# Inverse product over the 32 places on 64-row halves, with the correction added in the third stage

## The chip, the cores and the metric

One core of one Trainium2 chip runs the kernel. The metric is the device time of one execution in microseconds (us), as the median of several runs. The profile comes from one execution taken by the hardware profiler; its span (first to last instruction) is a little shorter than the time of that execution.

## The reference

The input x has 2048 rows of 576 numbers. After a layer norm the kernel adds three things: x itself, a spectral filter, and a gated linear unit.

```python
def _A_ref(x, w_r, w_i):
    X = rfft2(x, axes=(-2, -1))
    X = X * (w_r + 1j * w_i)
    return irfft2(X, s=(S, D), axes=(-2, -1))

def _B_ref(x, w_gate, w_up, w_down):
    g = einsum("bsd,df->bsf", x, w_gate)
    u = einsum("bsd,df->bsf", x, w_up)
    return einsum("bsf,fd->bsd", sigmoid(g) * u, w_down)

xn = _layernorm(x, axis=-1)
return x + _A_ref(xn, A_w_r, A_w_i) + _B_ref(xn, B_w_gate, B_w_up, B_w_down)
```

S is 2048, D is 576 and F is 4608. The setup scales w_r and w_i by 64.

## The kernel before

All matmuls run on numbers that are split in two: a high part with 12 bits and the rest, the low part. A product of two numbers is then three matmuls: high by high, high by low, low by high. Where the text speaks of a main sum and a correction, the correction is the part that comes from a matrix's low part.

The gated unit makes nearly all the work. It is cut into 36 blocks of 128 columns of F ("units"), and the 2048 rows into two halves of 1024, which run one after the other. A unit in `unit` has seven products of seven matmuls of 128x512 (`prod`, L710). Beside them run the down products `ps` (L1060) and `po` (L849) with 12 matmuls of 128x288 to a group.

The spectral filter is spread over the second half of the kernel. One step of it is done after each of the seven products of a unit; a step lasts some 2.7 us. The two-dimensional transform is done in three stages, and each task of a stage is a generator whose `yield`s are the ends of its steps:

- Stage one, `phase1b`, 16 tiles: the transform over the columns and then over the 64 slow places of the 2048 rows. It writes the result, high and low part apart, to `sc1` in the chip's main memory.
- Stage two, `phase2`, 16 tasks of 4.1 steps' distance: each takes four spectral rows (two pairs), transforms over the 32 fast places (`pb`, L566), multiplies by the filter `w` (the tile `ri`) and transforms back over the 32 places (`pc`, L591). The filtered numbers are split in `zh` and `zl` (128 partitions x 2 x 290). The result is evicted to `u` by ScalarE (L593) and written to `sc2` by a DMA on SyncE's queue (L594).
- Stage three, `phase3`, 16 tiles of 4.5 steps' distance: it loads a tile of `sc2` (L599), splits it into `uh` and `ul` (L612, L613), transforms back over the 64 places (`py`, L619), then over the columns (`pz`, `pe`), and adds the result to the output rows.

The constant `bm` holds four 128x128 matrices of stage two, two for the forward direction and the high and low part of the inverse one. In the inverse product the matmuls are full: for each of the two halves of `zh` and `zl`, three matmuls of 128 rows and 290 columns, so six in one task:

```python
pc = pair(f"pc{i}")
for j in range(2):
    for n, (k, m) in enumerate(((2, zh), (2, zl), (3, zh))):
        nc.tensor.matmul(pc[:, j, :NQ], bm[:, k, :], m[:, j, :], start=n == 0, stop=n == 2)
```

What sets the order: `pair` gives out two double PSUM banks in turn, to `pb`, `pc`, the sums `ps` and `po` and the products of stage three alike. A product can take its bank only when the one before it in that bank was evicted. TensorE takes its matmuls in the order in which they were laid out. All DMAs of the filter, as well as the weight pieces `w` (L323) and the down factors `wf` (L957), are issued on SyncE's queue, which works in order: a trigger that waits holds those behind it. In the second half the weights have one buffer, in which a piece is replaced as soon as its product is done and is read again one unit later. Instructions that are marked `keep_in_program_order` keep their place; others can be laid out earlier or later by the framework as their operands and buffers come free.

Of the kernel before, what the change touches and what calls it, by code (L numbers as in the profile page):

```python
# [9 lines left out]
F32 = mybir.dt.float32  # L10
F32R = mybir.dt.float32r
I32 = mybir.dt.int32
AF = mybir.ActivationFunctionType
# [3 lines left out]
P = 128  # L17
S, D, F = 2048, 576, 4608
KD = D // 2 + 1
NQ = KD + 1  # L20
# [36 lines left out]
def _split(m):  # L57

    def r12(v):
        b = np.ascontiguousarray(v, np.float32).view(np.uint32).astype(np.uint64)  # L60
        b = ((b + 0x7FF + ((b >> 12) & 1)) & 0xFFFFF000).astype(np.uint32)
        return b.view(np.float32)

    hi = r12(m.astype(np.float32))
    lo = r12((m - hi.astype(np.float64)).astype(np.float32))
    return hi, lo


def _cplx(m):

    return np.block([[m.real, m.imag], [-m.imag, m.real]])


def _constants():
    out = {}

    mid = np.arange(HD) - (D - 1) / 2
    ang = 2 * np.pi * mid[:, None] * KOF[None, :] / D
    t = np.zeros((P, 2, 5, NQ), np.float32)
    for e, v in ((0, np.cos(ang)), (1, -np.sin(ang))):  # L80
        m = np.where(FREQ, v - (v.mean(0) if e == 0 else 0), 0.0)
        hi, lo = _split(m)
        for part, w in ((0, hi), (1, lo)):
            t[:, e, 2 * part] = w[:P]
            t[:, e, 2 * part + 1] = w[P:2 * P]
        t[:KR, e, 4] = np.concatenate([hi[2 * P:], hi[2 * P:], lo[2 * P:]])
    out["cf"] = t.reshape(P, 10 * NQ)


    s1 = np.arange(N1)  # L90
    k1 = np.arange(N1)
    am = np.zeros((P, N2, 2, P), np.float32)
    ai = np.zeros((P, N2, 2, P), np.float32)
    for s2 in range(N2):
        ph = 2 * np.pi * (((N2 * s1[:, None] + s2) * k1[None, :]) % S) / S
        m = _cplx(np.exp(-1j * ph))
        am[:, s2, 0], am[:, s2, 1] = _split(m)
        m = _cplx(np.exp(1j * ph).T)
        ai[:, s2, 0], ai[:, s2, 1] = _split(m)
    out["am"] = am.reshape(P, N2 * 2 * P)  # L100
    out["ai"] = ai.reshape(P, N2 * 2 * P)


    s2 = np.arange(N2)
    ph = 2 * np.pi * ((s2[:, None] * s2[None, :]) % N2) / N2
    bh, bl = (v.reshape(2, N2, N1).transpose(1, 0, 2).reshape(N1, N1) for v in _split(_cplx(np.exp(-1j * ph))))
    none = np.zeros_like(bl)
    bi = _cplx(np.kron(np.exp(1j * ph), np.eye(2)))
    at = np.arange(P).reshape(2, N2, 2)
    bi = bi[at.transpose(2, 0, 1).ravel()][:, at.transpose(1, 0, 2).ravel()]  # L110
    b = np.stack([np.block([[bh, bl], [bh, none]]), np.block([[bl, bh], [none, bh]]), *_split(bi)], 1)
    out["bm"] = b.reshape(P, 4 * P)


    a = np.where((KOF == 0) | (KOF == HD), 1.0, 2.0)[:, None] / (D * S) * FREQ[:, None]
    ang = 2 * np.pi * KOF[:, None] * (QTR[None, :] + 0.5) / D
    t = np.zeros((P, 2, 2, 2, HQ), np.float32)
    r = np.zeros((P, 2, HD), np.float32)
    for e, m in ((0, a * np.cos(ang)), (1, a * np.sin(ang))):
        m[KOF == (HD, 0)[e]] = 0.0  # L120
        hi, lo = _split(m)
        for k, rows in enumerate((slice(0, P), slice(NQ - P, NQ))):
            t[:, e, k, 0], t[:, e, k, 1] = hi[rows], lo[rows]
        h, l = np.zeros((2, FR, HD), np.float32)
        for s, v in ((h, hi), (l, lo)):
            v = v[P:NQ - P]
            o = ODD[P:NQ - P]
            s[o, (1 - e) * HQ:(2 - e) * HQ] = v[o]
            s[~o, e * HQ:(e + 1) * HQ] = v[~o]
        r[:3 * FR, e] = np.concatenate([h, h, l])  # L130
    out["di"] = np.concatenate([t.reshape(P, 8 * HQ), r.reshape(P, 2 * HD)], 1)
    out["id"] = np.eye(P, dtype=np.float32)
    return out
# [6 lines left out]
def _layout(x, w_r, w_i, w_gate, w_up, w_down):  # L140

    ks = np.concatenate([np.arange(KT * P), np.tile(np.arange(KT * P, HD), 4)])
    w = np.stack([w_gate[COLS], w_up[COLS]]).reshape(2, 2, HD, NF, P)[:, :, ks]
    w = w[[1, 1, 0, 0], [0, 1, 1, 0]].reshape(4, KT + 1, P, NF, P).transpose(3, 2, 0, 1, 4)
    v = np.stack([w_r, w_i])[:, :, KOF].reshape(2, N2, 2, N2 // 2, 2, NQ).transpose(3, 2, 1, 0, 4, 5)
    v = np.broadcast_to(v[:, :, None], (N2 // 2, 2, 2, N2, 2, 2, NQ))
    x = x.reshape(S, D)[ROWS][:, COLS]
    xt = x[:, np.argsort(COLS)].reshape(NT, P, 2, HD)
    xt = np.stack([xt[:, :, 0], xt[:, :, 1, ::-1]], 2)
    xt = xt[..., ks].reshape(NT, P, 2, KT + 1, P).transpose(0, 4, 2, 3, 1)  # L150
    xg = x.reshape(NT, P, 2, HD)[TPP:, ..., ks].reshape(2, TPC, P, 2, KT + 1, P).transpose(0, 3, 5, 4, 1, 2).reshape(2, 2, P, (KT + 1) * CW)
    lay = {"x": x.reshape(NT, P, D), "xt": xt.reshape(NT, P, 2 * (KT + 1) * P), "xg": xg, "ri": v.reshape(N2 // 2, P, 4 * NQ),
           "w": w.reshape(NF, P, 4 * (KT + 1) * P), "wd": w_down[:, COLS].reshape(NF, P, D)}
    return {k: np.ascontiguousarray(a) for k, a in lay.items()}
# [9 lines left out]
def spectral_glu_kernel(ctx: ExitStack, tc: tile.TileContext, x, xt, xg, ri, w_in, w_down, out):  # L164
# [3 lines left out]
    def f32(ap):  # L168
        return ap.bitcast(F32)
# [6 lines left out]
    def pair(name):  # L176
        return ps.tile([P, 2, 512], F32, tag="pp", name=name, bufs=2)
# [21 lines left out]

    rowd = tc.dram_tile([2, NT, P], F32, name="rowd")  # L200
    sc1 = tc.dram_tile([2, N2 * P, NQ], F32, name="sc1")
    sc2 = tc.dram_tile([N2 * P, NQ], F32, name="sc2")
    spill = tc.dram_tile([TPP * P, D], F32, name="spill")
    wsp = [tc.dram_tile([P, NX * 5 * P], F32, name=f"wsp{f}") for f in range(NF)]
    wdsp = [tc.dram_tile([P, 2 * D], F32, name=f"wdsp{f}") for f in range(NF)]
# [342 lines left out]

    def phase2(i):
        pool, bm, zz = R["pool"], R["bm"], R["zz"]  # L550
        kl = 2 * i
        x2 = pool.tile([P, 2, 2, NQ], F32R, tag="x2", name=f"x2{i}", bufs=2)
        nc.sync.dma_start(f32(x2), sc1.rearrange("a (q h kl) n -> (a q) h kl n", h=2, kl=N2)[:, :, kl:kl + 2])
        w = pool.tile([P, 2, 2, NQ], F32, tag="ri", name=f"ri{i}", bufs=2)
        nc.sync.dma_start(w.rearrange("p a j n -> p (a j n)"), ri[i])
        wr, wi = w[:, 0], w[:, 1]
        yield
        yield
        yield
        half = slice(0, N1), slice(N1, P)  # L560
        s, c = (pool.tile([P, 2, NQ], F32, tag=f"s{h}", name=f"s{h}{i}") for h in range(2))
        for h, o in enumerate((s, c)):
            yield
            pb = pair(f"pb{i}_{h}")
            for j in range(2):
                nc.tensor.matmul(pb[:, j, :NQ], bm[:, h, :], x2[:, h, j, :], start=True, stop=True)  # L566
            nc.scalar.activation(o, pb[:, :, :NQ], AF.Copy)
        yield
        for h, o in enumerate((s, c)):
            nc.vector.tensor_tensor(s[half[h]], o[half[h]], o[half[1 - h]], op=OP.add)  # L570
        yield
        sw = pool.tile([P, 2, NQ], F32, tag="sw", name=f"sw{i}")
        for k in range(4):
            o, v = (slice(N2 * m, N2 * (m + 1)) for m in (k, k ^ 1))
            nc.scalar.activation(sw[o], s[v], AF.Copy, scale=-1.0 if k % 2 == 0 else 1.0)
        z = pool.tile([P, 2, NQ], F32, tag="z", name=f"z{i}")
        nc.vector.tensor_tensor(z, wr, s, op=OP.mult)
        yield
        nc.vector.tensor_tensor(sw, wi, sw, op=OP.mult)
        nc.vector.tensor_tensor(z, z, sw, op=OP.add)  # L580
        yield
        zh, zl = zz[i % len(zz)]
        nc.scalar.activation(zh, z, AF.Copy)
        yield
        nc.vector.tensor_tensor(zl, z, f32(zh), op=OP.subtract)
        yield
        yield
        pc = pair(f"pc{i}")
        for j in range(2):
            for n, (k, m) in enumerate(((2, zh), (2, zl), (3, zh))):  # L590
                nc.tensor.matmul(pc[:, j, :NQ], bm[:, k, :], m[:, j, :], start=n == 0, stop=n == 2)  # L591
        u = pool.tile([P, 2, NQ], F32, tag="u", name=f"u{i}", bufs=2)
        nc.scalar.activation(u, pc[:, :, :NQ], AF.Copy)  # L593
        nc.sync.dma_start(sc2.rearrange("(p kl) n -> p kl n", kl=N2)[:, kl:kl + 2], u)  # L594

    def phase3(t):
        pool, di, dr = R["pool"], R["di"], R["dr"]
        u = pool.tile([P, 2, NQ], F32, tag="u3", name=f"u3{t}", bufs=2)
        nc.sync.dma_start(u, sc2[2 * t * P:(2 * t + 2) * P].rearrange("(j p) n -> p j n", j=2))  # L599
        ai = pool.tile([P, 2, 2, P], F32R, tag="ai", name=f"ai{t}", bufs=2)  # L600
        load_r(ai, con["ai"][:, t * 4 * P:(t + 1) * 4 * P].rearrange("p (a h m) -> p a h m", a=2, h=2))
        if t < TPP:
# [3 lines left out]
            a = acc[t]  # L606
        yield
        yield
        yield
        uh = pool.tile([P, 2, NQ], F32R, tag="uh", name=f"uh{t}")  # L610
        ul = pool.tile([P, 2, NQ], F32R, tag="ul", name=f"ul{t}")
# [960 lines left out]
```

## Time and profile before

| what | value |
|---|---|
| median of 3 runs | 1375.23 us (1375.2 to 1375.95) |
| profiled execution, its own time | 1374.97 us |
| its span | 1373.2 us |
| stage two's `pc` matmuls, first to last start | 931.4 to 1101.9 us |
| stage three's `py` matmuls, first to last start | 1117.9 to 1340.1 us |
| evictions `u<-pc`, number and median | 16, 657 ns |

How to read the profile: a row of a group has the line of the kernel, the engine, the operation, the tile written and the tiles read, the shape (partitions x elements), the number of instructions, then the busy time in us and the mean time of one in ns, then the idle time of the engine ahead of them with what ended it. PE is TensorE's matmul, PEld its weight load, DVE VectorE, ACT ScalarE, SPq the DMA queue of SyncE. Rows of the timeline begin with the start and the length in us and end with the number of instructions merged. Rows of the waits end with us in total, times and the longest. The printed length of a matmul is modelled and overlaps the next one's; the time from start to start is what TensorE spends on it.

### The profile page before, as it was taken

Reading aid. Unit: us, or ns where it says so; the run is one execution under the profiler, and the core shown is the slowest. Engines: PE = TensorE matmul, PEld = TensorE weight load, DVE = VectorE, ACT = ScalarE, POOL = GpSimd, SP = SyncE. Lnnn points to the kernel's source line nnn. Section 1 sums busy time; section 2 is a strip of 40 time slices with the busy share of each in tenths; the row PEclk is TensorE's granted clock in tenths of the full one; section 3 lists DMA queues with packets and bytes.
Section 4 is the critical chain, followed back from the end, with each engine's and each line's share of the span. In section 5 each row is a group of like instructions: output and inputs, shape, how many; then the busy total and the mean of one; then the engine's idle time right before and its main releaser. Section 6 shows DMA issues by size and latency. Waiting matters only on the chain.

```text
span 1373.2 us, 20459 instructions
## 1 busy us (share of the span) xinstructions
PE 1360.3 (99%) x7656; PEld 1201.3 (87%) x7656; DVE 1069.9 (78%) x1555; ACT 776.1 (57%) x1228; POOL 3.3 (0%) x5
## 2 busy tenths in 40 slices
PE   8999999999999999999999999999999999999998
PEld 6888888888888888998888898988888888899887
DVE  7988888787878787999458668667878847777885
ACT  6644767677777767744245545447767634443432
POOL 0000000000000000000000000000000000000000
PEclk9999999999999999999999999999999999999999
DMA  7567786767676766595888878788989787775643
GB/s 258 200 250 284 267 317 251 287 261 267 266 268 260 274 262 256 212 316 179 286 261 269 264 242 251 217 310 304 307 303 314 231 280 254 225 236 174 197 147 87
DMA packets 127058, 346.56 MB, mean 252 GB/s; under 512 B 12816, under 2 KB 34096, under 8 KB 122224
## 3 DMA queue, kind: packets, MB, share of 16 engines
q1 hardware_dynamic: 125968, 343.94, 72.1%
q8 instruction: 61, 1.00, 0.3%
q10 hardware_dynamic: 992, 1.31, 0.3%
q14 instruction: 37, 0.30, 0.1%
HBM read 208.74 MB, written 136.46 MB: 251 GB/s over the span
## 4 chain that ended last, share of the span: by engine, by line
PE 88%; DVE 9%; ACT 2%; issue 1%; DMA 1%; DVEq 0%; ACTq 0%
PE pB L710 23%; PE ps L1060 22%; PE pE L710 15%; PE pA L710 14%; PE po L849 5%; PE pd L527 2%; PE pe L650 1%; PE pc L591 1%; PE py L619 1%; PE pa L543 1%; DVE acc L858 1%; PE pb L566 1%; DVE ys L825 1%; DVE w L284 1%; DVE hs L981 0%
## 5 line engine op out<-in xcount | busy, mean ns | idle before, releaser
L710 PE MATMUL pB<-X,w 128*128 128x512 f32 x1484 | 376.8, 392 | 1.0 <-ACT v L801 0.7
L1060 PE MATMUL ps<-wf,hs 128*128 128x288 f32 x2436 | 360.8, 295 | 1.2 <-DVE ev L655 1.2
L1060 PEld LDWEIGHTS ps<-wf,hs 128*128 128x128 f32 x2436 | 343.4, 188 | 16.4 <-ACT u L593 1.3
L710 PEld LDWEIGHTS pB<-X,w 128*128 128x128 f32 x1484 | 269.5, 188 | 52.5 <-ACT v L801 4.1
L710 PE MATMUL pE<-X,w 128*128 128x512 f32 x1064 | 269.3, 391 | 0.0
L710 PE MATMUL pA<-X,w 128*128 128x512 f32 (+1 forms) x1006 | 253.9, 389 | 0.7 <-ACT X L476 0.2
L710 PEld LDWEIGHTS pE<-X,w 128*128 128x128 f32 x1064 | 194.2, 188 | 35.7 <-DVE ys L803 0.4
L710 PEld LDWEIGHTS pA<-X,w 128*128 128x128 f32 x1006 | 182.3, 188 | 34.6 <-ACT g L798 0.9
L981 DVE TENSOR_TENSOR hs<-ys,hs 128x1024 fp32r<-128x1024 f32 (+1 forms) x105 | 124.7, 1187 | 39.6 <-ACT hs L978 38.5
L282 ACT ACTIVATE w<-raw 128x768 fp32r<-128x768 f32 (+1 forms) x106 | 100.3, 948 | 54.0 <-DVE raw L306 28.7
L978 ACT ACTIVATE hs<-ys 128x1024 fp32r<-128x1024 f32 (+1 forms) x105 | 108.0, 1028 | 24.7 <-PE ps L1060 19.1
L825 DVE TENSOR_TENSOR ys<-ys,g 128x1024 f32<-128x1024 f32 x67 | 81.9, 1223 | 3.7 <-DVE ys L823 0.5
L284 DVE TENSOR_TENSOR w<-raw,w 128x512 fp32r<-128x512 f32 (+1 forms) x106 | 81.7, 771 | 2.5 <-ACT w L282 2.3
L788 ACT ACTIVATE pB<-pA 128x512 f32<-128x512 f32 x68 | 39.6, 582 | 73.9 <-PE pA L710 71.6
L806 ACT ACTIVATE g<-pB 128x512 f32<-128x512 f32 x68 | 40.6, 597 | 65.2 <-PE pB L710 65.0
L803 DVE TENSOR_TENSOR ys<-v,pE 128x512 f32<-128x512 f32 x68 | 46.5, 684 | 39.1 <-ACT v L801 38.5
L974 DVE TENSOR_TENSOR ys<-ys 128x1024 f32<-128x1024 f32 (+1 forms) x60 | 71.1, 1185 | 0.6
L849 PEld LDWEIGHTS po<-wb,hp 128*128 128x128 f32 x468 | 65.0, 188 | 2.8 <-ACT hp L887 0.4
L849 PE MATMUL po<-wb,hp 128*128 128x288 f32 x468 | 67.1, 296 | 0.0
L795 ACT ACTIVATE v<-pB 128x512 f32<-128x512 f32 x68 | 40.5, 595 | 45.7 <-PE pB L710 45.3
L801 ACT ACTIVATE v<-pB 128x512 f32<-128x512 f32 x68 | 40.5, 596 | 40.8 <-PE pB L710 40.1
L823 DVE TENSOR_TENSOR ys<-v,pE 128x512 f32<-128x512 f32 x67 | 45.8, 684 | 22.2 <-PE pE L710 21.6
(185 smaller groups left out, 1583.2 us busy)
## 6 DMA issues: line engine op xcount, KB each, us to landing
w<-wsp SPq DMA_DIRECT2D x246, 320.0 KB, 3.9
wsp<-w SPq DMA_DIRECT2D x34, 2240.0 KB, 7.2
wf<-fsp SPq DMA_DIRECT2D x105, 288.0 KB, 4.3
fsp<-wf SPq DMA_DIRECT2D x98, 288.0 KB, 3.3
raw<-in_w SPq DMA_DIRECT2D x34, 768.0 KB, 6.6
x<-sc SPq DMA_DIRECT2D x16, 580.0 KB, 5.2
ri<-in_ri SPq DMA_DIRECT2D x16, 580.0 KB, 5.7
dt<-in_wd SPq DMA_DIRECT2D x32, 288.0 KB, 5.7
```

What stands on the lines that cost most here:

```text
L282: placed(nc.scalar.activation(o[:, :, :3, :], src, AF.Copy))
L284: placed(nc.vector.tensor_tensor(o[:, :, 3:, :], src[:, :, :KT, :], f32(o[:, :, :KT, :]), op=OP.subtract))
L710: strictly(nc.tensor.matmul(bank[:, cols], w[:, sw, :], X[:, x, sx, cols], start=start and j == 0, stop=stop and j == len(steps) - 1, skip ...
L803: nc.vector.tensor_tensor(y1, v[:, 1], bank["E"], op=OP.add)
L806: nc.scalar.activation(g[:, 1], bank["B"], AF.Sigmoid)
L823: nc.vector.tensor_tensor(place(u, 0), v[:, 0], bank["E"], op=OP.add)
L825: nc.vector.tensor_tensor(h, h, g, op=OP.mult)
L849: nc.tensor.matmul(pd[b], l, r, start=start, stop=stop)
L974: nc.vector.tensor_tensor(o, at(a), at(b), op=op)
L978: nc.scalar.activation(hs[:, :, 0], o, AF.Copy)
L981: nc.vector.tensor_tensor(hs[:, :, 1], o, f32(hs[:, :, 0]), op=OP.subtract)
L1060: nc.tensor.matmul(pd[:, s], h[:, g, a, m], w[:, g, b], start=q == 0 and not seeded, stop=q == len(parts_) - 1, skip_group_check=seeded)
```

## The change

The inverse product is done on the two halves of the partitions one by one: a matmul takes 64 rows of `zh` or `zl` (one spectral row each), and the 128 columns of its matrix are the 64 columns of the main sum beside the 64 columns of the correction. For `zh` these are the matrix's high and low part, for `zl` the high part and zeros. So a product has two matmuls, and there are four rows: eight matmuls of 64 rows in two batches of four, a step apart, each batch with its own PSUM pair, eviction and store. Main sum and correction go to two halves of `sc2`, which is twice as large. Stage three loads both and adds them on VectorE before the split, one step later than before. The four spectral rows of a task now lie one behind the other in `sc1`, and the filter is laid out to match. The task has one empty step less after its load.

```diff
+    ih, il = (v.reshape(N1, 2, N2).transpose(0, 2, 1).reshape(N1, N1) for v in _split(_cplx(np.exp(1j * ph))))
     none = np.zeros_like(bl)
-    bi = _cplx(np.kron(np.exp(1j * ph), np.eye(2)))
-    at = np.arange(P).reshape(2, N2, 2)
-    bi = bi[at.transpose(2, 0, 1).ravel()][:, at.transpose(1, 0, 2).ravel()]
-    b = np.stack([np.block([[bh, bl], [bh, none]]), np.block([[bl, bh], [none, bh]]), *_split(bi)], 1)
+    b = np.stack([np.block(v) for v in ([[bh, bl], [bh, none]], [[bl, bh], [none, bh]], [[ih, il]] * 2, [[ih, none]] * 2)], 1)
...
-    sc2 = tc.dram_tile([N2 * P, NQ], F32, name="sc2")
+    sc2 = tc.dram_tile([2, N2 * P, NQ], F32, name="sc2")
...
     def phase2(i):
-        kl = 2 * i
-        x2 = pool.tile([P, 2, 2, NQ], F32R, tag="x2", name=f"x2{i}", bufs=2)
-        nc.sync.dma_start(f32(x2), sc1.rearrange("a (q h kl) n -> (a q) h kl n", h=2, kl=N2)[:, :, kl:kl + 2])
+        x2 = pool.tile([P, 4, NQ], F32R, tag="x2", name=f"x2{i}", bufs=2)
+        nc.sync.dma_start(f32(x2), sc1.rearrange("a (q k) n -> (a q) k n", k=N1)[:, 4 * i:4 * i + 4])
...
-        yield
...
-                nc.tensor.matmul(pb[:, j, :NQ], bm[:, h, :], x2[:, h, j, :], start=True, stop=True)
+                nc.tensor.matmul(pb[:, j, :NQ], bm[:, h, :], x2[:, 2 * j + h, :], start=True, stop=True)
...
-        yield
-        pc = pair(f"pc{i}")
         for j in range(2):
-            for n, (k, m) in enumerate(((2, zh), (2, zl), (3, zh))):
-                nc.tensor.matmul(pc[:, j, :NQ], bm[:, k, :], m[:, j, :], start=n == 0, stop=n == 2)
-        u = pool.tile([P, 2, NQ], F32, tag="u", name=f"u{i}", bufs=2)
-        nc.scalar.activation(u, pc[:, :, :NQ], AF.Copy)
-        nc.sync.dma_start(sc2.rearrange("(p kl) n -> p kl n", kl=N2)[:, kl:kl + 2], u)
+            yield
+            pc = pair(f"pc{i}_{j}")
+            for n, (k, m) in enumerate(((2, zh), (3, zl))):
+                for h in range(2):
+                    nc.tensor.matmul(pc[:, h, :NQ], bm[half[h], k, :], m[half[h], j, :], start=n == 0, stop=n == 1)
+            u = pool.tile([P, 2, NQ], F32, tag="u", name=f"u{i}_{j}", bufs=2)
+            nc.scalar.activation(u, pc[:, :, :NQ], AF.Copy)
+            nc.sync.dma_start(sc2.rearrange("a (q k) n -> (a q) k n", k=N1)[:, 4 * i + 2 * j:4 * i + 2 * j + 2], u)
 
     def phase3(t):
         u = pool.tile([P, 2, NQ], F32, tag="u3", name=f"u3{t}", bufs=2)
-        nc.sync.dma_start(u, sc2[2 * t * P:(2 * t + 2) * P].rearrange("(j p) n -> p j n", j=2))
+        v = pool.tile([P, 2, NQ], F32, tag="v3", name=f"v3{t}")
+        for a, o in enumerate((u, v)):
+            nc.sync.dma_start(o, sc2[a, 2 * t * P:(2 * t + 2) * P].rearrange("(j p) n -> p j n", j=2))
...
+        yield
+        nc.vector.tensor_tensor(u, u, v, op=OP.add)
```

More of the change, by code (lines that the diff above doesn't have):

```diff
@@ L144, in _layout @@
     w = w[[1, 1, 0, 0], [0, 1, 1, 0]].reshape(4, KT + 1, P, NF, P).transpose(3, 2, 0, 1, 4)
-    v = np.stack([w_r, w_i])[:, :, KOF].reshape(2, N2, 2, N2 // 2, 2, NQ).transpose(3, 2, 1, 0, 4, 5)
+    v = np.stack([w_r, w_i])[:, :, KOF].reshape(2, N2, N2 // 2, 2, 2, NQ).transpose(2, 4, 1, 0, 3, 5)
     v = np.broadcast_to(v[:, :, None], (N2 // 2, 2, 2, N2, 2, 2, NQ))
```

## The prediction

> **What bounds the kernel now.** I read the page first: shares by engine, the chain of work, the costliest groups. Then I read the stretch in which the changed code runs: busy time by stretch, the waits in it, and the timeline of one changed product. Last came the DMA issues.
>
> ```profile
> span 1373.2 us, 20459 instructions
> PE 1360.3 (99%) x7656; PEld 1201.3 (87%) x7656; DVE 1069.9 (78%) x1555; ACT 776.1 (57%) x1228; POOL 3.3 (0%) x5
> PEclk9999999999999999999999999999999999999999
> PE 88%; DVE 9%; ACT 2%; issue 1%; DMA 1%; DVEq 0%; ACTq 0%
> ```
>
> TensorE is busy 99% of the span and carries 88% of the chain; its granted clock is full throughout. The profiled execution took 1374.97 us, 1.77 us more than its span; the median of the runs is 1375.23. All sums below are made against 1374.97.
>
> Stage two (the products over the 32 places) runs from about 930 to 1104 us, stage three from there to 1342, the tail after it. Columns of the next view: busy us of PE, weight loads, DVE, ACT, POOL with counts; clock; DMA share; GB/s.
>
> ```profile
> 930.00:1104.00 174.00, 173.44 (x975) 153.75 (x974) 137.16 (x171) 117.44 (x178) 0.00 (x0) 1.00 0.86 288
> 1104.00:1342.00 238.00, 236.77 (x1436) 212.37 (x1434) 178.95 (x269) 98.81 (x187) 0.00 (x0) 1.00 0.67 214
> ```
>
> In both stretches PE is busy over 99%, so a nanosecond less on TensorE is a nanosecond off the end, and work on ACT (67%, then 42%) or DVE (79%, then 75%) is paid only where TensorE waits for it. How little it waits, the waits show: the first two rows are of 930:1104, the next five of 1104:1342.
>
> ```profile
> PEld ps L1060 <- ACT u L593: 1.3, 6, 0.2
> PE pB L710 <- ACT v L801: 0.6, 1, 0.6
> PEld ps L1060 <- ACT v L801: 1.3, 1, 1.3
> PEld pe L650 <- ACT z3r L640: 1.2, 4, 0.5
> PEld pz L635 <- ACT rp L626: 0.4, 1, 0.4
> PEld po L849 <- DVE acc L858: 0.4, 1, 0.4
> PE ps L1060 <- DVE ev L655: 1.2, 2, 0.9
> ```
>
> Not one names a DMA.
>
> **The inverse product on TensorE.** Now it is six full matmuls of 290 columns. On the timeline of the last one:
>
> ```profile
> 1101.22 0.29 PE L591 MATMUL pc<-zh,bmt 128*128 128x290 f32 x1
> 1101.35 0.30 PE L591 MATMUL pc<-zl,bmt 128*128 128x290 f32 x1
> 1102.02 1.77 PE L710 MATMUL pB<-X,w 128*128 128x512 f32 x7
> 1103.63 1.75 PE L1060 MATMUL ps<-wf,hs 128*128 128x288 f32 x12
> ```
>
> From the first to the product behind them: 1102.02 - 1101.22 = 0.80 us, 0.133 each. (The printed 0.29 is the model's length of one; the start-to-start time is what it costs.) Sixteen such products: 12.8 us.
>
> After the change there are eight matmuls of 290 columns, each over 64 rows, in two batches of four a step apart. A batch runs rows 0-63, rows 64-127, rows 0-63, rows 64-127; the two halves take different rows of the moving operand, different weights and different PSUM banks. No 64-row matmul is in this trace. The nearest row is a 96-row one, the last of seven for each half of a transform:
>
> ```profile
> L527 PE MATMUL pd<-cf,fh 128*128 128x290 f32 x128 | 30.6, 297 | 0.7 <-DVE x1l L243 0.7
> L527 PE MATMUL pd<-cf,fh 96*128 96x290 f32 x32 | 9.5, 298 | 0.0
> ```
>
> Its length is that of a 128-row one: fewer rows alone buy nothing. So the bounds of a batch are: above, four in a row, 4 x 0.133 = 0.53 us; below, two pairs that each stream together, 2 x 0.133 = 0.27. Against 0.80 for the old six, two batches are +0.27 or -0.27 us, and over 16 products **+4.3 or -4.3 us**.
>
> Between them decides the weight load, of which there are eight where there were six. Where matmuls are short, the loads show their own pace:
>
> ```profile
> 1332.71 0.19 PEld L650 LDWEIGHTS pe<-dit,z3l 128*128 128x128 f32 x1
> 1332.82 0.19 PEld L650 LDWEIGHTS pe<-dit,z3h 128*128 128x128 f32 x1
> 1332.93 0.30 PEld L710 LDWEIGHTS pE<-X,w 128*128 128x128 f32 x2
> ```
>
> They start 0.11 us apart, behind matmuls of 144 columns, which at 0.133/290 a column would need only 0.07. So a load of 128 columns takes about 0.11 us of a path that takes one at a time. I take this for the halves too, since no row shows two loads side by side: the first pair's loads are hidden behind the 512-column product ahead of it, the second pair's end 0.11 and 0.22 us after the first pair starts, and its later matmul streams until 0.22 + 0.133 = 0.355. Two batches are 0.71 us, **0.09 less than now, -1.4 us over 16.** I take that value: it lies between the bounds, and it is the one that the row nearest to a weight load gives.
>
> The Trainium skill, "TensorE: Matmul & The Clock Gate", Part 3 (Packing small matmuls), says that matmuls on different row groups run beside each other and that weight loads overlap running matmuls only when the row group differs; by that alone the sum would be the lower bound, -4.3. No row here shows it. Against it stands "TensorEngine Tiling (Array Packing)", Key Properties, by which a change of the array's division (not of the tile in it) drains TensorE; it is the third rival below.
>
> **ACT: a second eviction.** pc was evicted once per product, now once per batch:
>
> ```profile
> L593 ACT ACTIVATE u<-pc x16: 654/657/661, 932.4 to 1102.2; 128x580 f32<-128x580 f32 x16
> ```
>
> Sixteen more at 0.657 us are 10.5 us, which take ACT from 117.4 to 128 of 174 us (74%). They lie beside the products. What shows through is the rotation of the two double banks: the row "ps <- ACT u" above is a sum that had to wait until such an eviction had freed its bank, 1.3 us in all. With twice the evictions I charge the same once more, **+1.3 us**; the ends are 0 and 3.5 (each new eviction costing the 0.2 us of the longest one: 16 x 0.22). Were the cover gone, 10.5.
>
> **DMA and the SP queue.** Per product one more store of 290 KB, per third-stage tile one more load of 290 KB (v3).
>
> ```profile
> sc<-u SPq DMA_DIRECT2D x15, 290.0 KB, 3.6
> x<-sc SPq DMA_DIRECT2D x12, 580.0 KB, 5.2
> u<-sc SPq DMA_DIRECT2D x16, 290.0 KB, 3.4
> SPq L594 <- ACT u L593: 24.4, 16, 2.2
> SPq L323 <- PE pB L710: 75.3, 45, 4.2
> ```
>
> In stage two 288 GB/s over 174 us are 50 MB; 16 x 0.297 MB add 9.5%: the DMA share goes from 0.86 to about 0.94. That still fits, so nothing is charged; if the cover were gone, each per cent over 1.0 would cost 1.7 us. The store's trigger waits on SP for its eviction, 24.4/16 = 1.5 us now, and twice as often after; queued behind it are the loads of the next unit's weights (L323) and of the down factors (L957). The weight pieces refill a buffer whose piece TensorE has just read (SP waits for pB, 75.3 us in all) and are read again only seven products later, some 19 us. Cost nothing. In stage three the share goes from 0.67 to 0.73. v3 has one buffer, so its next load waits for the add, which stands one or two steps ahead of it in the program; u and v are issued three steps (about 8 us) before the add and land in 3.4. Nothing again.
>
> **DVE: the add in stage three.** Same shape as the subtraction behind it:
>
> ```profile
> L613 DVE TENSOR_TENSOR ul<-u,uh x16: 751/754/765, 1113.1 to 1336.2; 128x580 fp32r<-128x580 f32 x16
> ```
>
> 16 x 0.754 = 12.1 us; DVE goes from 179 to 191 of 238 us (80%). The waits of TensorE for DVE in that stretch are 0.4 + 1.2 = 1.6 us; I charge **+0.3**, with the ends 0 and 1.6 (as much again). Without cover: 12.1.
>
> **Moved steps.** Stage two's first product comes one step earlier after its load, the second batch stays on the step that the old product had, so the last store and the first load of stage three keep their times. The shorter lead is safe: the last x2 load is issued at 1060.5 and lands within 6.8 us, its product runs after 1076:
>
> ```profile
> L553 SPq DMA_DIRECT2D x<-sc x16: 529/530/1341, 894.8 to 1060.5; - x16
> L566 PEldq EVENT_SEMAPHORE  x16: 51/51/51, 909.0 to 1076.9; - x16
> ```
>
> x2 in one run of four rows instead of two of two, and the reordered ri, move the same bytes: nothing. Stage three ends one step later; at the tail:
>
> ```profile
> 1351.97 0.83 DVE L661 TENSOR_TENSOR acc<-acc,ev 128x288 f32<-128x288 f32 x2
> 1352.92 0.69 DVE L803 TENSOR_TENSOR ys<-v,pE 128x512 f32<-128x512 f32 x1
> 1355.50 0.69 DVE L810 TENSOR_TENSOR ys<-ys,g 128x512 f32<-128x512 f32 x1 [1.89 <-ACT g L806]
> ```
>
> The last three adds of the transform (about 2.0 us on DVE) move behind L803, which ends at 1353.6, and end at 1355.6, where L810 wants to start at 1355.50: **+0.1 us**, at worst one more 0.75 us in front of it.
>
> **The sum:** -1.4 + 1.3 + 0.3 + 0.1 = +0.3 us, so 1374.97 + 0.3 = **1375.3 us**.
>
> **The rivals.**
> *All in parallel.* If both halves' weights also load side by side, the product gives -4.3 and the rest +1.7: -2.6, 1372.4 us; with every cover perfect, 1370.7. For it: the halves share no rows and no bank. Against it: no two loads overlap in any row here.
> *The change doesn't do what it says* (slower). If the 64-row matmuls run one after another like the 96-row one beside its neighbours, eight replace six: +4.3 + 1.7 = +6.0, 1381.0 us. It decides as soon as a 64-row matmul takes over 0.80/8 = 0.10 us of TensorE's time. For it: the 96-row row. Against it: that one shares its rows with the next, these don't.
> *The array must run empty on entering and leaving each batch* (slower). A matmul lasts 0.295 us by its row while the next starts after 0.133, so 0.16 us of it lies under its follower. If that is laid bare at both ends of 32 batches: 64 x 0.16 = 10.4 us, with -1.4 + 1.7 together +10.7, 1385.7 us; with half of that, 1380.5. It eats the gain of the best case from 4.3/64 = 0.07 us a change on. For it: there are twice as many batches as products. Against it: the passage from 512 to 290 to 288 columns above costs nothing (0.80 for six, and 1103.63 - 1102.02 = 1.61 for seven of 512). By the Trainium skill's rule on changing the division, this is what happens; no row here has such a change.
> *DMA fills up.* If the added 9.5% cost twice their bytes, stage two needs 1.05 of its time: 5% of 174 = 8.7 us, some 1384. Against it: no TensorE wait names a DMA.
>
> **Chances.** Forecast 0.38, all in parallel 0.28, one after another 0.15, emptying 0.14, DMA 0.05. A measurement of this kernel tells 0.2% (2.75 us) from no change. Faster by more: 0.17 of the parallel case and 0.06 of the forecast, 0.23. Within it: 0.11 of the parallel case, 0.27 of the forecast, 0.02 of a slight emptying, 0.40. Slower: 0.05 + 0.15 + 0.12 + 0.05 = 0.37. The range 1370.5 to 1382.0 holds the forecast, the parallel case with perfect covers, one-after-another and half an emptying; outside lie most of the emptying case, of DMA, and little else. Most chance lies on both sides of zero; the forecast's own range is 1372.5 to 1378 (its charges at their ends).
>
> **What would show it.** On the timeline of a batch, from its first matmul to the next line's first: 0.36 us is the forecast, 0.27 all in parallel, 0.53 one after another; more than that, or a gap before or after the batch, emptying. Rows 0-63 and 64-127 starting almost together show that the halves overlap; loads closer than 0.11 us show the parallel case. The row "ps <- ACT u" near 2.6 us tests the eviction; TensorE's waits for DVE after 1104 near 1.9 us test the add; a DMA share of 0.94 and 0.73 the transfers. A DMA among TensorE's waits, or an order of the sums in stage two that leaves TensorE idle for a bank, would make the prediction wrong.

## The result, and the profile after

The changed kernel takes 1385.45 us (median of 6 runs, 1384.85 to 1387.1) against 1375.22 before: ratio 1.0074, 95% interval 1.0061 to 1.0087. It is slower by 10 us, outside the range of 1370.5 to 1382.0. The profiled execution took 1384.9 us with a span of 1383.1, 9.9 more than before.

The page of the kernel after, then its busy time by stretch (us busy of PE, weight loads, DVE, ACT, POOL; clock; DMA share; GB/s):

```profile
span 1383.1 us, 20609 instructions
PE 1368.6 (99%) x7688; PEld 1194.9 (86%) x7688; DVE 1079.7 (78%) x1571; ACT 783.6 (57%) x1244; POOL 3.3 (0%) x5
PEclk9999999999999999999999999999999999999999
```

```profile
930.00:1104.00 174.00, 173.53 (x964) 141.59 (x963) 135.24 (x168) 121.75 (x188) 0.00 (x0) 1.00 0.90 304
1104.00:1342.00 238.00, 235.73 (x1418) 209.79 (x1417) 179.80 (x273) 98.74 (x185) 0.00 (x0) 1.00 0.75 240
```

TensorE is as full as before and the clock as high; it only has more to do. The weight loads in the first stretch fell from 153.75 to 141.59 us in the same 174 us: something leaves TensorE without loading. The timeline of the last product shows it, first the matmuls and then the weight loads:

```profile
1107.26 1.75 PE L711 MATMUL pA<-X,w 128*128 128x512 f32 x7
1108.94 0.40 PE L588 MATMUL pc<-zh,bmt 64*128 64x290 f32 x2
1109.18 0.30 PE L588 MATMUL pc<-zl,bmt 64*128 64x290 f32 x2
1109.41 1.86 PE L711 MATMUL pB<-X,w 128*128 128x512 f32 x7
1111.11 1.09 PE L1061 MATMUL ps<-wf,hs 128*128 128x288 f32 x7
```

```profile
1108.94 0.19 PEld L588 LDWEIGHTS pc<-zh,bmt 64*128 64x128 f32 x2 [0.35 <-issue]
1109.05 0.19 PEld L588 LDWEIGHTS pc<-zl,bmt 64*128 64x128 f32 x2
1109.40 0.76 PEld L711 LDWEIGHTS pB<-X,w 128*128 128x128 f32 x4 [0.17 <-issue]
```

Two matmuls in 0.40 us, where one of them alone is 0.398 long: the two halves run together, and so do their loads (two in 0.19, one of which is 0.183 long). That much is the best case of the prediction. But look at the borders. Seven matmuls of 512 columns took 1.60 us before; here it is 1.68 until the batch starts (+0.08). The first pair holds the next back for 0.24 us in place of 0.133 (+0.11): its load begins only when its matmul does. From the second pair to the product behind it 0.23 (+0.10), and that product's seven take 1.70 (+0.10): its first load, too, begins only when it does, after 0.17 us without any load. So a batch costs 1111.11 - 1107.26 - 2 x 1.60 = 0.65 us: 0.27 for two pairs and 0.39 for going in and out. Two batches are 1.30 us against 0.80 before, 16 x 0.50 = 8.0 us more. In all 32 batches the trace has 0.46 to 0.47 us from the first matmul to the next product (1109.41 - 1108.94 in this one), more than the forecast's 0.36, with the gaps ahead and behind that the prediction named as the sign of emptying. The pauses of the weight loads at both ends recur too. These are the longest two waits of TensorE's weight loads from 930 to 1104 us ("issue" means that the profile shows nothing that was waited for; `pb` is the product that often follows a batch):

```profile
PEld pc L588 <- issue: 9.2, 26, 0.4
PEld pb L562 <- issue: 4.1, 24, 0.2
```

To see where the rest lies I follow two matmuls through the traces, the 2451st and the 3011th of those that write pA, pB or pE; all kernels have the same of them in the same order. Before, they start at 892.3 and 1107.3 us, and between them lies stage two.

| stretch | before | after | difference |
|---|---|---|---|
| start to the 2451st | 892.3 | 891.8 | -0.5 |
| 2451st to 3011th: stage two | 214.9 | 222.9 | **+8.0** |
| 3011th to the end: stage three, tail | 265.9 | 268.4 | **+2.5** |

Stage two grew by just what the batches cost. The +2.5 lie in stage three and the tail. Among TensorE's waits from 1110 to 1342 us are these, where before had 1.2 for z3r and 0.4 for rp:

```profile
PEld pe L651 <- ACT z3r L641: 2.4, 4, 1.5
PEld pz L636 <- ACT rp L627: 1.0, 1, 1.0
PEld pz L633 <- ACT rp L627: 0.6, 1, 0.6
PE pe L651 <- ACT z3r L641: 1.0, 1, 1.0
```

The prediction had TensorE waiting 1.6 us for VectorE before and near 1.9 after. The view of this stretch lists no such wait; what grew are waits for ScalarE.

And the group of the added operation (busy, mean ns, then idle time of VectorE ahead of it and who ended it):

```profile
L609 DVE TENSOR_TENSOR u<-u,v 128x580 f32<-128x580 f32 x16 | 12.2, 760 | 10.4 <-DMA u<-sc 7.2 <-issue 2.2 <-DMA v<-sc 0.9
```

The add is as long as forecast (12.2 us in all), but VectorE stood idle another 10.4 us ahead of it, 8.1 of them until a load landed.

### The profile page after: what moved, and what is told of

Read it like the earlier page. It is cut to its first block, busy times and chain, and to the rows that moved or that the text cites. A ratio compares the mean times of both kernels' runs of the same rounds, so it can differ in the third digit from the quotient of the medians.

```text
span 1383.1 us, 20609 instructions
## 1 busy us (share of the span) xinstructions
PE 1368.6 (99%) x7688; PEld 1194.9 (86%) x7688; DVE 1079.7 (78%) x1571; ACT 783.6 (57%) x1244; POOL 3.3 (0%) x5
## 4 chain that ended last, share of the span: by engine, by line
PE 89%; DVE 7%; ACT 2%; issue 1%; DMA 1%; SPq 0%; DVEq 0%; ACTq 0%
PE pB L711 23%; PE ps L1061 22%; PE pE L711 15%; PE pA L711 15%; PE po L850 5%; PE pd L525 2%; PE pe L651 1%; PE pc L588 1%; PE pb L562 1%; PE pa L541 1%; PE py L620 1%; DVE ys L826 1%; DVE acc L859 1%; PE b L1137 0%; DMA u<-sc 0%
```

## The experiments

Theory D says that entering and leaving the 64-row form costs a fixed amount per batch. Theory L says that in that form no weight load is ever hidden. Rival O blames the evictions, stores and the add. All edits are to the changed kernel unless another is named. "Stage two" and "rest" are the last two stretches of the table above, in the profiled execution of each run, as differences to before. In the stretch ahead of these two no edit changes TensorE's work, and still the runs differ from before by -0.5 to +0.9 us there (e3 by +1.5). So differences under 1 us in these columns are not read as effects.

| run | median us | ratio to before, 95% | stage two | rest |
|---|---|---|---|---|
| after | 1385.45 | 1.0074 (1.0061 to 1.0087) | +8.0 | +2.5 |
| e1 zero rows | 1384.37 | 1.0062 (1.0045 to 1.0078) | +6.5 | +3.0 |
| e2 full rows | 1379.7 | 1.0028 (1.0018 to 1.0039) | +1.9 | +2.7 |
| e3 twice | 1401.1 | 1.0184 (1.0163 to 1.0204) | +21.6 | +4.2 |
| e4 half by half | 1386.92 | 1.0081 (1.0061 to 1.0101) | +8.2 | +3.3 |
| e5 full, no add | 1376.01 | 1.0006 (0.9997 to 1.0015) | +1.6 | -0.7 |
| e6 full, one eviction | 1376.4 | 1.0005 (0.9996 to 1.0015) | -1.0 | +2.0 |
| e7 full, add on GpSimd | 1380.26 | 1.0035 (1.0022 to 1.0048) | +1.7 | +3.1 |
| e8 e7 and a multiply on GpSimd | 1381.82 | 1.0046 (1.0031 to 1.0061) | +3.5 | +2.9 |
| e9 lean halves | 1381.65 | 1.0043 (1.0028 to 1.0058) | +7.2 | -0.9 |
| e10 lean zero rows | 1379.24 | 1.0025 (1.0015 to 1.0035) | +5.0 | -0.9 |
| e11 lean full rows | 1374.57 | 0.9991 (0.9981 to 1.0000) | -1.0 | -0.1 |
| e12 full, sum in stage two | 1380.46 | 1.0034 (1.0022 to 1.0046) | +4.7 | +0.2 |
| e13 full, load only | 1379.91 | 1.0027 (1.0017 to 1.0037) | +1.2 | +5.9 |
| e14 full, add only | 1379.16 | 1.0026 (1.0016 to 1.0037) | +1.2 | +1.4 |

### e1: the same matmuls on all 128 rows

```diff
-            for n, (k, m) in enumerate(((2, zh), (3, zl))):
+            for n, m in enumerate((zh, zl)):
                 for h in range(2):
-                    nc.tensor.matmul(pc[:, h, :NQ], bm[half[h], k, :], m[half[h], j, :], ...)
+                    nc.tensor.matmul(pc[:, h, :NQ], bm[:, 2 + 2 * n + h, :], m[:, j, :], ...)
```

> The changed kernel, but each of the eight matmuls takes all 128 rows, with a matrix whose other 64 rows are zero; evictions, stores and the add stay. Theory L (in the 64-row form a weight load is not hidden: a pair takes a load of 0.11 us and a stream of 0.13, and going in and out costs once more each): the batch becomes four matmuls of 0.133 = 0.53 us instead of 0.66, two of them 1.07 against 0.80 before; 16 x (1.07 - 1.32) = -4 us, about 1381. Rival D (the array empties only at both ends of a batch): the same, 1381. Rival O (not the matmuls but the second evictions, the stores and the add make the loss): no change, 1385.

The batch is what every theory said of four full matmuls, and the borders are gone. Its timeline:

```profile
1106.40 1.77 PE L711 MATMUL pA<-X,w 128*128 128x512 f32 x7
1108.01 0.43 PE L588 MATMUL pc<-zh,bmt 128*128 128x290 f32 x2
1108.28 0.43 PE L588 MATMUL pc<-zl,bmt 128*128 128x290 f32 x2
1108.55 1.76 PE L711 MATMUL pB<-X,w 128*128 128x512 f32 x7
1110.14 1.75 PE L1061 MATMUL ps<-wf,hs 128*128 128x288 f32 x12
```

1110.14 - 1106.40 - 2 x 1.60 = 0.54 us, against 0.65. Yet the time fell by 1.1 us, not 4: a miss for the number, and nearer to rival O's 1385 than to 1381. Rival O is answered by e2 and e9 below. A wait took part of it. Of TensorE's weight loads for the sums, first e1 (from 880 to 1110 us), then the kernel after (888 to 1112):

```profile
PEld ps L1061 <- ACT u L590: 3.5, 12, 0.4
```

```profile
PEld ps L1061 <- ACT u L590: 1.1, 6, 0.2
```

With the batch shorter, the sum behind it comes to its bank before the eviction is through: 2.4 us more. e10 below has the same matmuls without the second eviction (and without the additions of stage three), and there the wait is 0.8:

```profile
PEld ps L1060 <- ACT u L591: 0.8, 3, 0.3
```

So the second eviction does cost something, but in the changed kernel the slow batch covers most of it.

### e2: four full matmuls

The high part of a row and its low part lie one above the other, the matrices are `[[ih, il], [ih, none]]` and its mirror.

```diff
-        nc.scalar.activation(zh, z, AF.Copy)
+        for h, o in enumerate((zh, zl)):
+            nc.scalar.activation(o[half[h]], z[half[h]], AF.Copy)
...
-        nc.vector.tensor_tensor(zl, z, f32(zh), op=OP.subtract)
+        for h, o in enumerate((zh, zl)):
+            nc.vector.tensor_tensor(o[half[1 - h]], z[half[h]], f32(o[half[h]]), op=OP.subtract)
...
+            for h, o in enumerate((zh, zl)):
+                nc.tensor.matmul(pc[:, h, :NQ], bm[:, 2 + h, :], o[:, j, :], start=True, stop=True)
```

> The changed kernel, but the high part of a spectral row and its low part lie one above the other on 128 rows, so that one full matmul does what two of 64 rows did: four per product in two batches of two, no 64-row matmul. It costs one more ACT copy and one more DVE subtract per product (16 x 0.68 and 16 x 0.76 us, beside TensorE). Theories L and D: a product takes 4 x 0.133 = 0.53 us against 0.80 before: 1375.2 - 4.3 and 1 to 2 us for evictions and the tail, 1372 to 1373. Rival O: the loss stays and grows by the added ACT and DVE work, 1385 or more.

1379.7: 5.8 us below the changed kernel, so the matmuls' form was the larger part of the loss; but 4 us above before and not 2 to 3 below. A batch is 0.27 us (two of them 0.53, 4.3 us less than before in all):

```profile
1104.04 0.29 PE L589 MATMUL pc<-zh,bmt 128*128 128x290 f32 x1
1104.18 0.30 PE L589 MATMUL pc<-zl,bmt 128*128 128x290 f32 x1
1104.31 1.78 PE L712 MATMUL pB<-X,w 128*128 128x512 f32 x7
```

But stage two is 1.9 us longer. The waits of its weight loads in 930 to 1104, the three longest:

```profile
PEld pB L712 <- ACT v L803: 3.4, 7, 1.2
PEld ps L1062 <- ACT u L591: 3.0, 11, 0.7
PEld pb L562 <- DVE ys L827: 1.0, 1, 1.0
```

Before had 0.8 and 1.3 in the first two and no third. What TensorE gained, it gave back waiting, for ACT above all.

### e3: every batch twice in a row

```diff
-            for n, (k, m) in enumerate(((2, zh), (3, zl))):
+            for n, (k, m) in enumerate(((2, zh), (3, zl)) * 2):
```

> The changed kernel with the four matmuls of a batch done twice over in a row (the second time writes the same numbers). Theory L: each further pair costs load and stream, 0.24 us; 64 more pairs, +15 us, about 1400. Rival D: inside a batch the loads are hidden and a further pair costs its stream, 0.133: +8.5, about 1394. Rival O: TensorE is not what counts there, under +3.

The total of 1401 is what theory L said, but the timeline of a batch says D:

```profile
958.01 0.40 PE L588 MATMUL pc<-zh,bmt 64*128 64x290 f32 x2
958.26 0.29 PE L588 MATMUL pc<-zl,bmt 64*128 64x290 f32 x2
958.39 0.29 PE L588 MATMUL pc<-zh,bmt 64*128 64x290 f32 x2
958.52 0.29 PE L588 MATMUL pc<-zl,bmt 64*128 64x290 f32 x2
958.75 0.54 PE L562 MATMUL pb<-x,bmt 128*128 128x290 f32 x2
```

Only the first pair holds its follower 0.25 us; then the pairs come 0.13 apart, and the step to the full matmul is 0.23 again. **Within the 64-row form, the loads are hidden and two matmuls cost what one full one does. The 0.39 us are paid at its two ends.** Theory L falls. So 64 more pairs are 64 x 0.133 = 8.5 us; stage two grew by 13.6 over the changed kernel. The other 5.1 are about the size of one wait, once more the eviction that holds the next sum:

```profile
PEld ps L1061 <- ACT u L590: 6.6, 11, 0.7
```

That is 5.5 more than the 1.1 of the changed kernel. A time alone would have taught the wrong theory here.

### e4: the order of the halves

```diff
-            for n, (k, m) in enumerate(((2, zh), (3, zl))):
-                for h in range(2):
+            for h in range(2):
+                for n, (k, m) in enumerate(((2, zh), (3, zl))):
```

> The changed kernel with the order of a batch changed: both matmuls of rows 0-63, then both of rows 64-127. Theory L, strict (a load waits for every running matmul): four turns of 0.24 us, +0.48 a batch, +15 us, about 1400. Theory L, by rows (a load waits only for the matmul that runs on its own rows): the middle two overlap, three turns, +0.24 a batch, +8, about 1393. Rival D: four streams of 0.133 at most, +0.07 to 0.27 a batch, 1387 to 1394, without a pause of 0.11 between the matmuls. Rival O: no change.

Theory L's 1393 and 1400 are out; 1386.9, within 1.5 us of the changed kernel, lies beside the lower edge of rival D's 1387 to 1394 and near rival O's "no change". It decides nothing between these, for the order did not come about. In the program as built the instructions stand as zh, zl for one half, then zh, zl for the other, yet the timeline has both zh first, in all 32 batches (the two loads of a pair start 6 to 7 ns apart, 3 to 4 in the changed kernel, so the two streams do differ):

```profile
1108.06 1.76 PE L711 MATMUL pA<-X,w 128*128 128x512 f32 x7
1109.75 0.40 PE L588 MATMUL pc<-zh,bmt 64*128 64x290 f32 x2
1109.99 0.29 PE L588 MATMUL pc<-zl,bmt 64*128 64x290 f32 x2
1110.21 1.92 PE L711 MATMUL pB<-X,w 128*128 128x512 f32 x7
```

TensorE started the other half's first matmul ahead of this half's second. The one overtaken sits on the rows that the matmul ahead of it was using; that this is why it was held is an inference.

### e5 to e8: what e2 lost beside its matmuls

e5 leaves out the second load and the add of stage three (and so the correction). e6 evicts only the first batch and stores it twice (the second batch's result is missing). e7 does the add on GpSimd, e8 also the first multiply with the filter.

```diff
e5:
-        for a, o in enumerate((u, v)):
+        for a, o in enumerate((u,)):
...
-        nc.vector.tensor_tensor(u, u, v, op=OP.add)
e6:
+            if j == 0:
                 nc.scalar.activation(u, pc[:, :, :NQ], AF.Copy)
e7:
+        nc.gpsimd.tensor_tensor(u, u, v, op=OP.add)
e8:
+        nc.gpsimd.tensor_tensor(z, wr, s, op=OP.mult)
```

> The full-row version (e2) without the second load and the add of stage three; the correction of the inverse matrix is left out of the result. Theory S (of what e2 lost beside its matmuls, the second eviction and the fuller ACT and DVE in stage two cost most, the add in stage three the lesser part): 1 to 3 us less than e2, 1377 to 1379, TensorE's pauses in stage two unchanged. Rival T (the add in stage three is the main loss, by DVE's lateness for the sums and the transposes): 4 us or more less, 1375.5 or below.

> The full-row version (e2) with only the first of the two batches of a product evicted and stored twice; the second batch's result is left out of the output. The matmuls, the stores and stage three stay. Theory S: the second eviction goes from ACT and from the banks' rotation, the waits of TensorE for ACT in stage two (about 8 us with e2) halve: 3 to 4 us less, 1376. Rival T: under 1 us less.

> The full-row version (e2) with the add of stage three on GpSimd, which is idle there, in place of VectorE. Theory S: no more than what e5 gains, 1 to 2.5 us, about 1378. Rival T: 4 us, about 1375.5, below the kernel before.

> As e7, and of stage two's product with the filter the first multiply (0.76 us on VectorE, 16 times) on GpSimd too. Theory S, if VectorE's fullness is part of it: 1 to 2 us less than e7, 1376 to 1377. If it is ACT's evictions alone: as e7. Rival T: as e7.

e5 is 3.7 us below e2, with the gain in the rest (+2.7 to -0.7) and not in stage two: between the two theories. e6 is 3.3 us below, 2.9 of it in stage two (+1.9 to -1.0), as theory S said. So each of the two additions alone costs the full-row version about 3.5 us. The two don't simply add up: e11 below takes out both and comes 5.1 us below e2, not 7.0. e7 was wrong for both: the add leaves VectorE and nothing comes back. It takes 1.45 us on GpSimd in place of 0.76, with no other work there in stage three. So VectorE's time alone does not explain what the add costs; that the longer add took back a gain isn't excluded. e8 is a miss too, 1.6 us slower than e7, and why is not shown.

### e9 to e11: the three forms of the product without the additions

One eviction per product, no second load, no add; the second batch's result and the correction are missing in all three. The edits are those of e5 and e6, on the changed kernel, on e1 and on e2.

> The changed kernel without its additions around the matmuls: the first batch alone is evicted (and stored twice), stage three has neither the second load nor the add. The second batch's result and the correction are left out of the output. Theory D (entering and leaving the 64-row form costs 0.39 us a batch, so two batches cost 1.32 us against the 0.80 of before): 16 x 0.52 = 8.3 us over before stay, 1383 to 1385. Rival M (the form of the matmuls counts for less, the loss is the evictions, stores and the add): 1379 or less.

> e9 with the matmuls of e1: all 128 rows, half of the matrix zero; the same parts are left out. Theory D: eight matmuls of 0.133 against six, +4.3, 1379 to 1381, some 4 us below e9. Rival M: within 1.5 us of e9.

> e9 with the four full matmuls of e2; the same parts are left out. Theory D: -4.3 and the added ACT copy and DVE subtract (0 to 2 us), 1371 to 1373.5, below before and some 12 us below e9. Rival M: within 3 us of e9.

The order is theory D's: halves +5.7 us over before, zero rows +3.3, full rows -1.4. In stage two, where the product is, it is +7.2, +5.0 and -1.0, against +8.0, +4.3 and -4.3 by the matmuls alone. So halves and zero rows stand where their matmuls put them within a microsecond, and rival M falls (it had 1379 or less for the halves, and e11 within 3 us of them). Two of theory D's three totals are missed all the same: 1381.65 where it had 1383 to 1385, 1374.57 where it had 1371 to 1373.5. The rest of the time, without the additions, is 0.9 us shorter than before's in e9 and e10, which no forecast had. And the full form stands 3.3 us above its matmuls, for it meets other waits, as in e2. In 880 to 1110 us of e11:

```profile
PEld pB L711 <- ACT v L802: 1.6, 5, 0.5
PEld pb L562 <- DVE qs L995: 1.2, 3, 0.6
```

### e12: the correction added in stage two

```diff
-            nc.scalar.activation(u, pc[:, :, :NQ], AF.Copy)
+            nc.scalar.activation(u[:N1], pc[N1:, :, :NQ], AF.Copy)
+            nc.vector.tensor_tensor(u[:N1], pc[:N1, :, :NQ], u[:N1], op=OP.add)
```

> The full-row version (e2) with the correction added at once: ACT copies its 64 rows out of PSUM, VectorE adds the main sum from PSUM on the way out. One store of half the size, stage three as before but for its extra step. VectorE has 0.75 us more twice per product in stage two, 24 us, and the bank is held for copy and add, 1.4 us. Theory D with fuller banks and VectorE: no gain over e2, 1378 to 1382. If the stores, the second load and the add of stage three were the larger part: 1375 or below.

As expected of the fuller banks: the rest is nearly that of before (+0.2), stage two +4.7. The work only moved. No version that computes the whole result beat the kernel before.

### e13 and e14: the halves of the addition in stage three

e13 keeps the second load of e2 and drops the add; e14 keeps an operation of the add's shape (the maximum of the tile with itself) and drops the load. Both leave the correction out.

```diff
e13:
-        nc.vector.tensor_tensor(u, u, v, op=OP.add)
e14:
+        nc.vector.tensor_tensor(u, u, u, op=OP.max)
```

> The full-row version (e2) with the second load of stage three but without the add; the correction is left out of the output. Theory W (the add's place costs: it waits for a landing at the head of an in-order queue, and what stands behind it in stage three comes late): as e5, 1376 to 1377. Rival Q (the second load costs, by the queue of SyncE and the DMA share): as e2, 1379 to 1380.

> The full-row version (e2) without the second load, with an operation of the add's shape on VectorE in its place that leaves the numbers as they are (the maximum of the tile with itself); the correction is left out of the output. Theory W: as e2, 1379 to 1380. Rival Q: as e5, 1376 to 1377.

Not settled. e14 keeps most of e2's loss (1379.2; single runs from 1378.0 to 1380.7), as theory W has it, and TensorE's weight loads wait for the same things as in e2 (from 1110 to 1342 us):

```profile
PEld pz L636 <- ACT rp L627: 1.4, 1, 1.4
PEld pe L651 <- ACT z3r L641: 1.3, 4, 0.5
```

But e13 is as slow (1379.9; single runs from 1376.8 to 1382.2), by a wait that neither e2 nor the changed kernel shows, once for 3.7 us:

```profile
PEld pA L711 <- DMA w<-wsp: 3.7, 1, 3.7
```

The profiled execution of e13 took 1382.15, 2.2 us above the median, so its +5.9 stands for the long runs. Without a reader, the second load waits on SyncE's queue for the landing of the one before it, and the weights queue behind it (from 1110 to 1340 us):

```profile
SPq L599 <- DMA v<-sc: 23.1, 6, 5.1
```

With e2 this wait is 0.4 us in all; the experiment made a cost of its own. What can be said: the add's operation is enough to bring most of the loss, and the load alone brings another of like size in another place.

## Why the prediction was wrong

**The bound** was right: TensorE full, clock full, no wait of TensorE for a DMA in stage two of the kernel after. What the matmuls cost went straight into the time: 8.0 by the rows of a batch, 8.0 in the stretch.

**The step that failed** is the product: "the first pair's loads are hidden behind the 512-column product ahead of it", and with it a free way in and out. -1.4 us was forecast, +8.0 came. Both ends of the batch cost: 0.08 + 0.11 going in, 0.10 + 0.10 going out. The prediction's other assumption there, that loads go one at a time at 0.11 us, was wrong as well, but in the kernel's favour: both halves load together. By the rows of e3 a pair costs 0.133, so the product would have been the -4.3 of the parallel case if it had no ends. Nor does a load wait for matmuls on its own rows, the condition beside that case: within e3's runs of pairs each load, on rows that were in use, was hidden.

**The third rival** comes nearest: a price at both ends of 32 batches, 0.16 us each, 1385.7 us; measured 0.39/2 = 0.19 an end, and 1385.45. It had a chance of 0.14. That its total came so close is luck in part: the ends cost 2.1 us more than its 10.4, the pairs 2.9 less than its -1.4, and the evictions, the add and the tail some 0.8 more than its 1.7. And about half of an end (0.11 going in, 0.10 going out) is a weight load that begins only with its matmul, which this rival did not name. The reason against it was the weak point: that 512, 290 and 288 columns follow each other for nothing shows a change of size, and the rival spoke of a change of the array's division, of which the trace had no row. A row that doesn't contain the thing is no evidence against it. The Trainium skill, "TensorEngine Tiling (Array Packing)", Key Properties, has the rule without a price: changing the division drains TensorE. The trace agrees as far as a price goes, 0.19 us a change; that the array runs empty no row shows by itself.

**The second eviction**, +1.3: little in the changed kernel, where the wait is 1.1 us as it was 1.3 before; without it (e9) stage two is 0.8 us shorter, too little to be read as an effect. It hides behind the slow batches; with the fast ones of e2 it is worth 2.9 us in stage two (e2 against e6).

**The add**, +0.3: mis-sized. The rest is 2.5 us longer than before. Without the additions of stage three it is 3.4 us shorter in e9 against the changed kernel, 3.4 in e5 against e2 and 3.9 in e10 against e1 (e9 and e10 lack the second eviction too). The sum costed the add by VectorE's free time and left out that VectorE stands idle ahead of it until a load lands, 8.1 us in all. That this delay, passed on to ScalarE's z3r and rp, is what TensorE waits for is the likeliest reading and not shown: e7 shows only that moving the add to a free engine doesn't help. How the cost divides between the load and the add stays open.

**Transfers and moved steps**: no charge, and no wait of TensorE for a transfer in stages two and three of the kernel after. The DMA share is 0.90 and 0.75 (0.94 and 0.73 forecast). But "Nothing again" for the two loads of stage three did not hold for VectorE, as said under the add. The extra step at the tail cost nothing that shows: e5, e9 and e10 have it, and their rest is shorter than before's.

**One sum** of the prediction does not come out: with its charges at their ends (0 to 3.5, 0 to 1.6, 0.1 to 0.75) and the product at -1.4, the forecast's own range is 1373.7 to 1379.4, not 1372.5 to 1378. Nothing else hangs on it.

## What to carry to other kernels

Matmuls on half the rows ran two at a time, but each run of them between full matmuls paid 0.39 us for its ends here: two pairs in place of three full matmuls save 0.13 and lose 0.39. By these numbers, as an estimate for 290 columns, a run of pairs comes out ahead only where it replaces over 0.39/0.133 = 3 full matmuls more than it has pairs; both batches of a product in one run, 4 x 0.133 + 0.39 = 0.92 us, would still lose against 0.80. No run tried a longer one against the full matmuls it replaces. Filling the rows instead (high and low part one above the other, e2) got the gain on TensorE without ends, and then the next limit decided: the evictions and adds that the new form needed. No gain was left: the best of these versions, e11, is 1.4 us below before, with an interval that ends at 1.0000, and leaves part of the result out. When a trace holds no instance of what a change introduces, its rule should stand as a case of like weight with the forecast, however cleanly other transitions pass.

## What had not been expected of the hardware

Weight loads for the two halves start together and end together (two in 0.19 us), where the loads for all 128 rows, in the prediction's rows, start 0.11 us apart. TensorE does not always take its matmuls in the order in which they were laid out, as the text on the kernel before has it: with e4 a matmul on other rows started ahead of the one before it, in all 32 batches. And a shorter batch can lay bare a wait that the longer one had covered: the sum's wait for the eviction was 1.1 us with the slow batches, 3.5 with e1's.
